# Attention, then two expert layers, on one core: the opening of the attention written out as a sequence of its own

## The chip, the core and the metric

The kernel runs on one core of a Trainium2 chip. TensorE (PE in the rows) multiplies matrices into PSUM. VectorE (DVE), ScalarE (ACT) and GpSimd (POOL) work on SBUF; the first two also read PSUM. SyncE (SP), ACT and POOL issue transfers, which run on 16 DMA engines. Each engine works through its own list in order and waits on semaphores for the others. The metric is the device time of one execution in microseconds (us); the median of several runs is compared.

## What is computed

Inputs q, k, v have shape (2, 8, 576, 64): 16 heads of 576 positions by 64 numbers; s has shape (2, 8, 576). The result of the attention goes through two expert layers (1152 tokens, 8 experts, 512 to 1024 to 512). Only the attention is touched here:

```python
scores = scale * np.matmul(q, k.transpose(0, 1, 3, 2))
s_pos = np.maximum(s, 0.0)
cum = np.cumsum(s_pos, axis=-1)
bias = -(cum[:, :, :, None] - cum[:, :, None, :])
scores = np.where(causal, -1000000000.0, scores + np.minimum(bias, 0.0))
scores = scores - np.max(scores, axis=-1, keepdims=True)
attn = np.exp(scores)
attn = attn / (np.sum(attn, axis=-1, keepdims=True) + 1e-09)
return np.matmul(attn, v)
x = _moe_ref(x=x, **moe_kwargs)      # first expert layer
return _moe2_ref(x=x, **moe2_kwargs) # second expert layer
```

## The kernel before, in words

The 16 heads come as 8 pairs n, heads 2n and 2n+1; a head's 576 positions are five tiles of 128 (the last holds 64). Four things happen to a head m:

- **Turning** (T, TE). The pair's q and k are split into two float16 numbers each, high on ACT (`split_q`, `split_k`, line 401) and low on DVE (line 441). TensorE transposes the tiles into PSUM (line 452), ACT copies them out (line 409): `AL` is the turned k, `AR` the turned q. `AL` is also copied to the lower half of `BLS` by a transfer on SP's queue (line 463); the upper half of `BLS` holds a fixed pattern of 32-column groups.
- **Maxima** (M, D, G). TensorE forms the scores in four pieces u = 0 to 3 (`m_pe`, line 476; the causal mask is added by line 478 from `mask_ij`), DVE adds the decays `CB[m]` and takes the row maxima into `rm` (`m_dve`, line 488). `CB[m]` is row m of the running sums `cum13`, the same on all 128 partitions. ACT rounds `rm` (`q_dve0`, line 494, task G0), POOL forms the difference `ng` to the references `refb` and splits it into `QB` (`q_dve1`, task G1). A piece's PSUM tile is one of two, so piece u+2 waits for DVE's maximum of piece u.
- **Exponentials** (Q, QE, E). `QB` is turned on TensorE and copied by DVE into `BR`; TensorE forms the scores again, turned (lines 528 to 531), ACT takes the exponential into `pf` (line 536).
- **Values** (P, V, R, X). DVE and POOL split `pf` into two halves (lines 403 and 414), TensorE multiplies with v (lines 559 to 564), DVE divides; per pair the rows are turned and multiplied with the gate weights of the first expert layer.

One loop runs over m from -7 to 18. In each step two written lists, one for even and one for odd m (`ORDER`), set the order in which these tasks are issued for different heads: E for m, Q for m+1, M, D and G for m+3, T for m+5, K for the pair (m+7)/2. The steps of negative m are the fill: they run the same lists with the tasks whose head does not exist yet left out. Beside the lists stand `filled(m)` (paddings, set by POOL), `references()` at m = -5 (from `cum13`, the references `refb` and the exponents' offsets `XB`) and `groups()` at m = -3 (the pattern in `BLS[0]`, made by DVE, and five transfers from POOL's queue that copy it to the other five `BLS`). `cum13` is a scan on DVE over `s` (lines 303 and 305); it is written to DRAM, and `cum_load(m)` reads row m back onto 128 partitions, 288 KB a head.

SP's queue takes, in program order, s, k and q of each pair (each in three transfers: `load_qkv`, lines 207 and 208), the decays, v, the gate weights and the copies into `BLS`. At m = 10 the gate of the first half of the tokens is taken, and from there on weights of the expert layers arrive; the two expert layers follow.

Of the kernel before, what the change touches and what calls it, by code (L numbers as in the profile page):

```python
# [21 lines left out]
def tile_attention_moe_moe(ctx: ExitStack, tc: tile.TileContext, q, k, v, s, wg1, w1a, w2a, capacity,  # L22
                           wg2, w1b, w2b, out, dbg=None):
    nc = tc.nc
# [196 lines left out]
    load_qkv(KF, k, 1)  # L221

    for l in (KF, QF):
        nc.gpsimd.memset(l[0][64:, 4], 0.0)
    gi = sp.tile([P, S], I32, name="gi")

# [4 lines left out]
    VH = [ap.tile([P, NS16, 2, D + 1], F16, name=f"vh{i}") for i in range(3)]  # L231
    ALS, ARS = ([ap.tile([P, SW], F16, name=f"{n}{i}") for i in range(6)] for n in ("al", "ar"))
    BLS = [ap.tile([P, SW], F16, name=f"bl{i}") for i in range(6)]
    xt = ap.tile([P, 2, SW], F16, name="xt")
    RMS = [ap.tile([P, NT], F32, name=f"rm{i}") for i in range(4)]
# [5 lines left out]
    def filled(m):  # L241

        put = nc.gpsimd.memset
        if m == -6:
            for l in (KF, QF):
                put(l[1][64:, 4], 0.0)
        if m == -5:
            nc.gpsimd.iota(gi[64:96], pattern=[[1, S]], base=0, channel_multiplier=-32)
        if m in (-4, -2):
            for i in range(3):  # L250
                for x in (ALS, ARS, BLS):
                    put(x[i + 3 * (m == -2)][:, S:], 0.0)
        if m == -4:
            for x in RMS:
                put(x, 0.0)
            for l in (KF, QF):
                put(l[2][64:, 4], 0.0)
        if m == -3:
            for i in range(2):
                put(VF[i][64:, 4], 0.0)  # L260
                put(VF[i][:, :, :, D:], 32.0)
            for x in VH:
                put(x[:, :, :, D:], 32.0)
            put(QB[0][:, :, :, D:], 0.0)
        if m == -2:
            put(QB[1][:, :, :, D:], 0.0)
        if m in (-2, -1):
            i = m + 2
            put(PFS[i][:, NCOL:], 0.0)
            put(PFS[i][64:, NCOL - 64:NCOL], 0.0)  # L270
            for l in (PHS, PLS):
                put(l[i][:, 2 * S - P:], 0.0)
        if m == -1:
            put(QB[2][:, :, :, D:], 0.0)
            put(zero[:, :DM + E + 1], 0.0)
            put(zero[:, DM + E + 1:], 2e6)
        if m == 0:
            for i in range(2, 4):
                put(VF[i][64:, 4], 0.0)
                put(VF[i][:, :, :, D:], 32.0)  # L280
# [51 lines left out]
    magic = ap.tile([P, 1], F32, name="magic")  # L332
    nc.vector.memset(magic, MAGIC)

    def groups():
        nc.vector.tensor_scalar(g1[64:96], gi[64:96], 0.0, -1024.0, op0=OP.is_ge, op1=OP.mult)
        for r in (64, 96):
            nc.vector.scalar_tensor_tensor(BLS[0][r:r + 32, :S], gi[64:96], 31.0, g1[64:96], op0=OP.is_le, op1=OP.mult)
        for x in BLS[1:]:
            nc.gpsimd.dma_start(x[64:, :S], BLS[0][64:, :S])  # L340

    def references():
# [1673 lines left out]
```

## Time and profile before

| what | value |
|---|---|
| median of 3 runs | 454.91 us (452.60 to 456.92) |
| the profiled execution, its own time | 451.49 us |
| its span, first to last instruction | 449.7 us |
| PE / DVE / ACT / POOL busy, share of the span | 88% / 74% / 58% / 42% |
| scan done (start of the attention's own work on DVE) | 5.47 us |
| first maximum of head 0 / 1 / 2 / 3 on DVE | 13.69 / 20.10 / 25.90 / 31.49 us |
| first exponential's matmul, head 0 | 28.74 us |
| last of the attention's values | about 141 us |

The times are of one execution. A row of the timeline gives the start, the duration, the engine and line, what is written from what, and in square brackets how long the engine stood idle before it and who released it. Busy shares are means over stages with different limits, so the opening is read by itself.

### The profile page before, as it was taken

What the parts mean: (1) busy time and instruction counts of PE and PEld (TensorE: products, weight loads), DVE (VectorE), ACT (ScalarE), POOL (GpSimd) and SP (SyncE); (2) the same over time, 40 slices, a digit from 0 to 9 for tenths busy, and PEclk for the clock granted to TensorE, in tenths of its full rate; (3) what the DMA queues carried; (4) which work ended last, traced back from release to release, by engine and by line L of the source; (5) the groups of instructions that cost most, each with busy time, mean ns of one, the idle gap of its engine ahead of it and who ended that gap; (6) DMA issues with size and microseconds to landing.
All of it is one profiled execution on the core that took longest, in us unless ns stands there. A gap on an engine that the chain in (4) does not pass through costs nothing. (4 is left out here: it accounts for less than half of the span.)

```text
span 449.7 us, 13971 instructions
## 1 busy us (share of the span) xinstructions
PE 397.8 (88%) x5378; PEld 366.1 (81%) x5378; DVE 330.9 (74%) x954; ACT 262.2 (58%) x473; POOL 190.9 (42%) x306
## 2 busy tenths in 40 slices
PE   1679999975987799999999999868979999999992
PEld 1447888864876699999999999737969999999991
DVE  7889999984667466776778894767598878877620
ACT  4457898752574165555556854533486776675631
POOL 4387888867470512052044081420254233334221
PEclk9979999998899999999999999998999999999997
DMA  7797999777924769999999691096999898899411
GB/s 156 168 214 171 224 227 199 189 180 243 362 30 158 250 202 318 355 347 339 336 341 377 101 175 21 20 264 155 331 366 332 272 336 279 260 336 315 143 42 32
DMA packets 94399, 103.04 MB, mean 229 GB/s; under 512 B 56136, under 2 KB 63304, under 8 KB 94323
## 3 DMA queue, kind: packets, MB, share of 16 engines
q1 hardware_dynamic: 88931, 91.85, 70.9%
q0 software_dynamic: 4192, 9.91, 7.4%
q8 instruction: 44, 0.72, 0.7%
q10 hardware_dynamic: 1200, 0.30, 0.3%
q14 instruction: 32, 0.26, 0.2%
HBM read 81.42 MB, written 14.59 MB: 213 GB/s over the span
## 5 line engine op out<-in xcount | busy, mean ns | idle before, releaser
L164 DVE TENSOR_TENSOR wl<-wf,wh 128x1024 bf16<-128x1024 f32 x64 | 78.0, 1237 | 20.8 <-ACT wh L160 19.2
L160 ACT ACTIVATE wh<-wf 128x1024 f16<-128x1024 f32 x64 | 65.7, 1050 | 16.8 <-issue 9.1
L937 PE MATMUL A<-xt,wl 128*128 128x144 f16 (+4 forms) x288 | 59.5, 231 | 0.0
L935 PE MATMUL A<-xt,wh 128*128 128x144 f16 (+4 forms) x288 | 59.5, 231 | 0.0
L936 PE MATMUL A<-xt,wh 128*128 128x144 f16 (+4 forms) x288 | 59.5, 231 | 0.0
L992 PE MATMUL C<-h,wf 128*128 128x160 f32 (+7 forms) x544 | 58.3, 269 | 0.0
L1107 POOL DMA_INDIRECT x2d<-xo,tix x14 | 22.9, 1637 | 74.1 <-DVE l L1124 26.4
L937 PEld LDWEIGHTS <-wl 128*128 128x128 bf16 x512 | 50.2, 98 | 1.5 <-issue 1.5
L936 PEld LDWEIGHTS <-wh 128*128 128x128 f16 x512 | 50.2, 98 | 1.4 <-issue 0.9
L935 PEld LDWEIGHTS <-wh 128*128 128x128 f16 x512 | 50.3, 98 | 1.2 <-PE pM L652 1.0
L536 ACT ACTIVATE pf<-pE,XB 128x512 f32<-128x512 f32 (+4 forms) x80 | 36.8, 514 | 12.5 <-PE pE L531 12.4
L488 DVE CUSTOM_DVE_ANT_0 junk<-pM,cb 128x128 f16<-128x128 f32 (+4 forms) x80 | 32.2, 431 | 11.7 <-PE pM L478 11.0
L1885 POOL DMA_INDIRECT out_dram<-x2f,tok x14 | 16.8, 1198 | 55.9 <-ACT h L943 24.9
L414 POOL TENSOR_TENSOR pl<-pf,ph 128x512 f16<-128x512 f32 x30 | 35.5, 1194 | 9.2 <-DVE ph L403 7.5
L476 PE MATMUL pM<-al,ar 128*128 128x128 f16 (+2 forms) x96 | 27.9, 330 | 11.6 <-DVE rm L488 7.0
L164 DVE TENSOR_TENSOR wf<-wf,wf 128x1024 bf16<-128x1024 f32 x30 | 35.7, 1219 | 2.6 <-ACT wf L160 2.6
L992 PEld LDWEIGHTS C<-h,wf 128*128 128x128 f32 x256 | 36.2, 190 | 0.0
L1454 POOL DMA_INDIRECT xg<-x2d,tok x16 | 24.0, 1498 | 23.4 <-PE A L1152 11.0
L1865 PE MATMUL C<-h,wf 128*128 128x144 f32 (+1 forms) x312 | 32.0, 257 | 0.0
L160 ACT ACTIVATE wf<-wf 128x1024 f16<-128x1024 f32 x30 | 31.3, 1052 | 0.0
L559 PE MATMUL pog<-vf,pf 128*128 128x65 f32 x180 | 29.4, 287 | 0.0
L937 PE MATMUL C<-xt,wl 128*128 128x144 f16 x128 | 24.6, 226 | 0.0
(415 smaller groups left out, 1188.8 us busy)
## 6 DMA issues: line engine op xcount, KB each, us to landing
wf<-in_moe_w_dram SPq DMA_DIRECT2D x128, 512.0 KB
xd<-zero SPq DMA_DIRECT2D x18, 257.0 KB
cb<-cumd SPq DMA_DIRECT2D x16, 288.0 KB
x2d<-zero SPq DMA_DIRECT2D x9, 260.5 KB
kf<-in_k_dram SPq DMA_DIRECT2D x16, 128.0 KB
vf<-in_v_dram SPq DMA_DIRECT2D x16, 128.0 KB
qf<-in_q_dram SPq DMA_DIRECT2D x14, 128.0 KB
bl<-al SPq DMA_DIRECT2D x16, 72.0 KB
```

Of the source, the lines that this page charges most:

```text
L160: nc.scalar.activation(hi, src, AF.Copy)
L164: nc.vector.tensor_sub(lo, src, hi)
L414: (nc.gpsimd if ENG[name][i % 2] == "P" else nc.vector).tensor_sub(o, x, y)
L476: nc.tensor.matmul(o, AR[m][:, t * P:(t + 1) * P], AL[m][:, j0:j1], start=True, stop=not diag)
L488: nc.vector.tensor_tensor_reduce(junk[:w, :j1 - j0], o, CB[m][:w, j0:j1], 1.0, r if t == 4 and j0 == 0 else -3e38, OP.add, OP.max, r)
L536: nc.scalar.activation(d, o, AF.Exp, bias=x, scale=2.0 ** -13)
L559: nc.tensor.matmul(o, pf[:, c:c + P], VF[n % 4][:, j, h], start=False, stop=j == t)
L935: nc.tensor.matmul(ph[:, g], wh[:, c, fs], xt[:, c], start=c == 0, stop=False)
L936: nc.tensor.matmul(ph[:, g], wh[:, c, fs], xt[:, 4 + c], start=False, stop=False)
L937: nc.tensor.matmul(ph[:, g], wl[:, c, fs], xt[:, c], start=False, stop=c == 3)
L992: nc.tensor.matmul(py[:, g], a[:, f, d], b[:, f], start=k == 0, stop=k == len(terms) - 1)
L1865: nc.tensor.matmul(py[:, g], a[:, f, d], b[:, f], start=k == 0, stop=k == len(terms) - 1)
```

## The change

The loop starts at m = -1. What its steps -7 to -2 did is written out as straight code ahead of it, in another order and with other means:

- k of a pair comes in one transfer: partition p holds nine neighbouring rows of the pair, 2304 bytes in one piece, where before 256-byte rows were spread over three transfers. The pair is turned by nine transposes instead of ten, and ACT puts the columns back in place with two strided copies (a first of 640, a second of 512 elements a partition) that serve both heads.
- The decays of heads 0, 1 and 2 no longer come from DRAM: a float32 matmul spreads the row of `cum13` over 128 partitions (512 and 64 columns), and ACT copies it from PSUM (`cum_pe`). Heads 3 to 15 still load them.
- The references' work on DVE follows the scan at once, ahead of k's and q's low halves; `refb` is made by ACT. The masks are made by DVE after that, where before they stood ahead of the scan. The group pattern is made ahead of the scan, one piece instead of two; two POOL transfers (5 and 6 heads, 32 partitions each) copy it.
- Paddings are merged into fewer, larger memsets and stand early on POOL. v of pairs 0 and 1 and both layers' gate weights are loaded from POOL's queue instead of SP's, between these paddings.
- `G0` (the rounding of `rm`) moves behind the last maximum, `D3`, in both lists and in the fill. Head 0's turned q is copied by DVE instead of ACT.

```diff
@@ load_qkv, filled (was called by m, now by steps)
+        if l is KF:
+            queue.dma_start(x, r.rearrange("h (q t) d -> (h q) t d", t=NK))
+            return
...
+        if step == 0:
+            put(ABL[:, :, S:], 0.0)
+            put(RMA, 0.0)
+            put(QF[1][64:, 4], 0.0)
+            put(VHS[:, :, :, :, D:], 32.0)
...
+            nc.gpsimd.dma_start(wgf, wg1.rearrange("(c p) e -> p c e", p=P))
+            for n in range(2):
+                load_qkv(VF, v, n, nc.gpsimd)
+            nc.gpsimd.dma_start(wg2f, wg2.rearrange("(c p) e -> p c e", p=P))
+            put(QB[0][:, :, :, D:], 0.0)
+            put(QF[2][64:, 4], 0.0)
+        if step == 1:
+            for r, i in ((64, 1), (96, 0)):
+                nc.gpsimd.dma_start(ABL[r:r + 32, 12 + i:, :S], BLS[0][64:96, None, :S].to_broadcast([32, 6 - i, S]))
...
-    load_qkv(QF, q, 1)
-    cum_load(0)
-    cum_load(1)
...
+    def cum_pe(m):
+        CB[m] = aw.tile([P, S], F32, name="cb", bufs=3)
+        for c0, c1 in ((0, 512), (512, S)):
+            pb = psE.tile([P, 512], F32, name="pE")[:, :c1 - c0]
+            nc.tensor.matmul(pb, identf[:NH, m:m + 1].to_broadcast([NH, P]), cum13[:, c0:c1], start=True, stop=True)
+            nc.scalar.activation(CB[m][:, c0:c1], pb, AF.Copy)
...
-        for r in (64, 96):
-            nc.vector.scalar_tensor_tensor(BLS[0][r:r + 32, :S], gi[64:96], 31.0, g1[64:96], op0=OP.is_le, op1=OP.mult)
-        for x in BLS[1:]:
-            nc.gpsimd.dma_start(x[64:, :S], BLS[0][64:, :S])
...
-        nc.vector.tensor_scalar(refb, pr, MAGIC, None, op0=OP.add)
+        nc.scalar.activation(refb, pr, AF.Identity, bias=magic)
@@ t_evac
-        moved("AL", m, AL[m][:, :S], ps[0][:, :S])
-        moved("AR", m, AR[m][:, :S], ps[1][:, :S])
+        for p, t0 in zip(ps[:-1], (0, NT)):
+            t1 = min(t0 + NT, NK)
+            nc.scalar.activation(ABL[:, m % 6:m % 6 + 2, :S].rearrange("p h (q t) -> p h q t", t=NK)[:, :, :, t0:t1],
+                                 p[:, :(t1 - t0) * P].rearrange("p (t h q) -> p h q t", h=2, t=t1 - t0), AF.Copy)
+        if m:
+            moved("AR", m, AR[m][:, :S], ps[-1][:, :S])
+        else:
+            raw_copy(AR[m][:, :S], ps[-1][:, :S])
@@ the opening
-    for m in range(-7, NH + 3):
+    filled(0)
+    references()
+    split_k(0)
+    split_rest()
+    split_q(0)
+    masks()
+    split_rest()
+    cum_pe(0)
+    refs = references_pe()
+    turned0 = t_pe(0)
+    split_k(1)
+    t_evac(0, turned0)
+    split_rest()
+    references_out(*refs)
+    filled(1)
+    maxima(0, {0: lambda: turn(1), 1: lambda: split_q(1), 2: lambda: cum_pe(1)})
...
+    gate_weights()
+    split_v(0)
+    maxima(1, {0: lambda: turn(2), 1: split_rest, 2: lambda: (split_k(2), cum_pe(2))})
+    cum_load(3)
+    load_v(2)
+    split_v1(0)
+    split_rest()
+    split_q(2)
+    turn(3)
+    split_rest()
+    filled(3)
...
+    for m in range(-1, NH + 3):
```

What stands in the lists of three engines is shown at the three places that matter most. On DVE, before, right behind the scan (the second row) come k's and q's low halves of pair 0 and k's of pair 1, and only then the references:

```order
L303 TENSOR_SCALAR srow<-srow 16x576
L305 SCALAR_TENSOR_TENSOR cum<-ones_row,srow 16x576
L333 MEMSET magic 128x1
L441 SCALAR_TENSOR_TENSOR ka<-kf_109,ka 128x10x64
L403 COPY qa<-qa 128x10x64
L441 SCALAR_TENSOR_TENSOR qb_132<-qf_108,qa 128x10x64
L441 SCALAR_TENSOR_TENSOR ka<-kf_112,ka 128x10x64
L344 TENSOR_SCALAR ref_263<-cum 16x18
```

Now the group pattern (`abl<-gi`) stands ahead of the scan and the references right behind it; k's low half comes last of these:

```order
L295 SCALAR_TENSOR_TENSOR abl<-gi,g_152 32x576
L298 TENSOR_SCALAR srow<-srow 16x576
L300 SCALAR_TENSOR_TENSOR cum<-ones_row,srow 16x576
L341 TENSOR_SCALAR ref_211<-cum 16x18
L342 TENSOR_SCALAR ref_211<-ref_211 16x18
L343 CAST refh<-ref_211 16x18
L345 TENSOR_TENSOR r8l<-ref_211,refh 16x18
L346 CAST refh<-r8l 16x18
L347 TENSOR_TENSOR selc<-ident 64x16
L348 SCALAR_TENSOR_TENSOR ones_row<-ref_211,cum 16x576
L443 SCALAR_TENSOR_TENSOR ka<-kf_109,ka 128x9x64
```

On TensorE, between the third and the fourth piece of head 0's scores, two float32 matmuls now stand (they spread head 1's decays; the last row is the fourth piece, whose maximum ends head 0):

```order
L491 MATMUL pM<-abl 128x512
L493 LDWEIGHTS identk
L493 MATMUL pM<-mask_ij,identk 128x128
L321 MATMUL pE<-cum,identf 128x512
L321 MATMUL pE<-cum,identf 128x64
L491 LDWEIGHTS abl
L491 MATMUL pM<-abl 128x512
```

On POOL, ahead of head 0's difference to the references (`ng`, in both lists), eight transfers now stand that were on SP's queue, and the two copies of the pattern. The rows start behind the last padding of v's second pair:

```order
L259 DMA wgf<-in_moe_w_gate_dram 128x4x8
L211 DMA vf_110<-in_v_dram 128x4x64 x2
L212 DMA vf_110<-in_v_dram 64x2x64
L211 DMA vf_113<-in_v_dram 128x4x64 x2
L212 DMA vf_113<-in_v_dram 64x2x64
L262 DMA wg2f<-in_moe_w_gate_dram 128x4x8
L263 MEMSET qb_131 128x10x64
L264 MEMSET qf_114 64x128
L267 DMA abl<-abl 32x5x576
L267 DMA abl<-abl 32x6x576
```

Before, only paddings stood ahead of that difference on POOL, and the pattern's copies came behind it:

```order
L263 MEMSET vh_137 128x4
L264 MEMSET qb_132 128x10x64
L500 TENSOR_TENSOR ng<-rm_157,refb 128x90
L403 CAST qb_132<-ng 128x5x18
L414 TENSOR_TENSOR qb_132<-ng,qb_132 128x5x18
L340 DMA bl_151<-bl_150 64x576
```

## Rows read from the trace of the kernel before

**Rows 1.** Busy time by stretch: length, five engines (instructions), granted clock, DMA share, GB/s.
```profile
5.47:31.49 26.02, 15.78 (x130) 11.59 (x130) 20.48 (x60) 13.07 (x27) 12.69 (x41) 0.87 0.85 185
31.49:90.94 59.45, 57.89 (x849) 49.44 (x848) 57.44 (x201) 49.19 (x113) 49.06 (x72) 1.00 0.87 202
27.30:30.70 3.40, 3.40 (x22) 2.35 (x22) 2.40 (x6) 2.81 (x5) 2.95 (x11) 0.50 0.99 228
```

**Rows 2.** Timeline of DVE in the opening: start, duration, what; idle before, released by.
```profile
1.60 0.17 DVE L62 MEMSET ones<- 128x128 f16 x1
...
3.01 1.07 DVE L303 TENSOR_SCALAR srow<-srow 16x576 f32<-16x576 f32 x1 [0.18 <-DMA srow<-in_s_dram]
4.12 1.35 DVE L305 TENSOR_TENSOR_SCAN cum<-ones_row,srow 16x576 f32<-16x576 f32 x1
...
6.90 0.82 DVE L441 SCALAR_TENSOR_TENSOR ka<-kf,ka 128x640 f16<-128x640 f32 x1 [1.43 <-ACT ka L401]
...
11.77 0.46 DVE L363 TENSOR_SCALAR refb<-pM 128x288 f32<-128x288 f32 x1 [0.79 <-PE pM L360]
...
13.69 0.29 DVE L488 CUSTOM_DVE_ANT_0 junk<-pM,cb 128x128 f16<-128x128 f32 x1 [0.46 <-issue]
...
17.85 0.50 DVE L336 TENSOR_SCALAR g<-gi 32x576 f32<-32x576 int32 x1
18.38 1.58 DVE L338 SCALAR_TENSOR_TENSOR bl<-gi,g 32x576 f16<-32x576 int32 x2
...
23.43 1.82 DVE L405 TENSOR_SCALAR vf<-vf 128x640 f32<-128x640 f32 x1
...
31.49 0.29 DVE L488 CUSTOM_DVE_ANT_0 junk<-pM,cb 128x128 f16<-128x128 f32 x1 [1.42 <-PE pM L478]
...
35.91 0.77 DVE L405 TENSOR_SCALAR vf<-vf 128x640 f32<-128x640 f32 x1
...
48.19 0.48 DVE L405 TENSOR_SCALAR vf<-vf 128x640 f32<-128x640 f32 x1
```

**Rows 3.** Timeline of PE: the references, the turn at m = -1, and float32 matmuls.
```profile
10.54 0.66 PE L357 MATMUL pM<-identf,ones_row 16*128 16x16 f32 x5 [1.51 <-DVE ones_row L347]
11.13 0.60 PE L360 MATMUL pM<-refh,selc 64*128 64x18 f16 x16
...
12.70 0.31 PE L476 MATMUL pM<-al,ar 128*128 128x128 f16 x1
...
27.29 0.59 PE L476 MATMUL pM<-al,ar 128*128 128x512 f16 x1
27.68 0.74 PE L452 MATMUL pT<-ident,ka 128*128 128x128 f16 x5
...
28.74 0.63 PE L528 MATMUL pE<-br,bl 128*128 128x512 f16 x1
...
110.35 1.52 PE L559 MATMUL pog<-vf,pf 128*128 128x65 f32 x6
111.67 0.63 PE L476 MATMUL pM<-al,ar 128*128 128x512 f16 x1
```

**Rows 4.** Timeline of ACT: a copy of turned k in the fill; the end of an even step (m = 2).
```profile
8.54 0.65 ACT L409 ACTIVATE al<-pT 128x576 f16<-128x576 f16 x1 [0.41 <-PE pT L452]
...
46.42 0.30 ACT L494 ACTIVATE rm<-rm,magic 128x5 f32<-128x5 f32 x1
...
...
49.28 0.84 ACT L536 ACTIVATE pf<-pE,XB 128x64 f32<-128x64 f32 x2 [0.79 <-PE pE L531]
```

**Rows 5.** Timeline of POOL: transfers that it issues, and head 0's difference.
```profile
17.18 0.85 POOL L500 TENSOR_TENSOR ng<-rm,refb 128x90 f32<-128x90 f32 x1 [11.39 <-DVE rm L488]
...
20.28 2.85 POOL L340 DMA_DIRECT2D bl<-bl  x5 [0.93 <-DVE wgh L370]
...
105.77 0.98 POOL L706 DMA_INDIRECT xd<-XR,slot  x1 [0.30 <-issue]
107.06 0.93 POOL L706 DMA_INDIRECT xd<-XR,slot  x1 [0.30 <-issue]
```

More of the change, by code (lines that the diff above doesn't have):

```diff
@@ L221, in tile_attention_moe_moe @@
     load_qkv(KF, k, 1)
-    for l in (KF, QF):
-        nc.gpsimd.memset(l[0][64:, 4], 0.0)
+    load_qkv(QF, q, 1)
     gi = sp.tile([P, S], I32, name="gi")
+    nc.gpsimd.iota(gi[64:96], pattern=[[1, S]], base=0, channel_multiplier=-32)
+    nc.gpsimd.memset(QF[0][64:, 4], 0.0)
     SW = NT * P
@@ L239, in tile_attention_moe_moe, with filled @@
     XSS = [ap.tile([P, NT, 2, D], F32, name=f"xs{i}") for i in range(2)]
-    def filled(m):
+    def filled(step):
         put = nc.gpsimd.memset
[L244 to L258, printed above, removed]
-            for i in range(2):
[L260 to L274, printed above, removed]
@@ L276, in filled @@
             put(zero[:, DM + E + 1:], 2e6)
[L277 to L280, printed above, removed]
+        if step == 3:
+            for x in VF[2:]:
+                put(x[64:, 4], 0.0)
+                put(x[:, :, :, D:], 32.0)
             put(xt[:, :, S:], 0.0)
@@ L353, in references, with references_pe @@
         nc.vector.tensor_copy(refh[32:32 + NH], r8l)
-        pb = psM.tile([P, NT, NH], F32, name="pM")
+        nc.vector.tensor_tensor(selc, ident[:64, :NH], ident[:64, 32:32 + NH], OP.add)
+        nc.vector.scalar_tensor_tensor(xrow.rearrange("e (g w) -> e g w", w=32),
+                                       ref8[:, :, None].to_broadcast([NH, G, 32]), -1024.0,
+                                       cum13.rearrange("e (g w) -> e g w", w=32), op0=OP.mult, op1=OP.add)
+    def references_pe():
+        pr = pog[:, :NH * G].rearrange("p (h g) -> p h g", g=G)
+        pb = pog[:, NH * G:NH * G + NT * NH].rearrange("p (t h) -> p t h", h=NH)
+        for h in range(NH):
+            nc.tensor.matmul(pr[:, h], selc[:, h:h + 1].to_broadcast([64, P]), refh, start=True, stop=True)
         for t in range(NT):
@@ L456, in t_pe @@
         n, h, b, hh = heads(m)
-        return [transposed(KA[n][:, :, h]), transposed(QA[n][:, :, h])]
+        ps = []
+        for t0 in (0, NT) if h == 0 else ():
+            p = psT.tile([P, SW], F16, name="pT")
+            for t in range(t0, min(t0 + NT, NK)):
+                nc.tensor.transpose(p[:, (t - t0) * P:(t - t0 + 1) * P], KA[n][:, t], ident)
+            ps.append(p)
+        return ps + [transposed(QA[n][:, :, h])]
     def t_evac(m, ps):
+        n, h, b, hh = heads(m)
         AL[m], AR[m] = ALS[m % 6], ARS[m % 6]
-        moved("AL", m, AL[m][:, :S], ps[0][:, :S])
-        moved("AR", m, AR[m][:, :S], ps[1][:, :S])
+        for p, t0 in zip(ps[:-1], (0, NT)):
[6 more added lines that the diff above has]
+            raw_copy(AR[m][:, :S], ps[-1][:, :S])
         nc.sync.dma_start(BLS[m % 6][:64, :S], AL[m][:64, :S])
@@ L758, in tile_attention_moe_moe, with maxima, turn @@
     ORDER = [
-        "E0 Q E1 K X1 M0 D0 V0 M1 V1 D1 X QE M2 VS XE E3 P0 D2 P1 QS E2 V2 R0 R1 G0 M3 T R2 D3 XG VT TE L LG G1 LV S".split(),
-        "E0 VS M0 V0 Q D0 M1 E1 D1 P0 P1 V1 X1 E3 K E2 QE M2 V2 D2 R0 M3 X T R1 G0 LG XE TE R2 D3 QS L S G1 VT XG LV".split(),
+        "E0 Q E1 K X1 M0 D0 V0 M1 V1 D1 X QE M2 VS XE E3 P0 D2 P1 QS E2 V2 R0 R1 M3 T R2 D3 G0 XG VT TE L LG G1 LV S".split(),
+        "E0 VS M0 V0 Q D0 M1 E1 D1 P0 P1 V1 X1 E3 K E2 QE M2 V2 D2 R0 M3 X T R1 LG XE TE R2 D3 G0 QS L S G1 VT XG LV".split(),
     ]
     made = {}
-    for m in range(-7, NH + 3):
+    def maxima(m, between):
+        for u in range(4):
+            m_dve(m, m_pe(m, u))
+            if u in between:
+                between[u]()
+        q_dve0(m)
+        q_dve1(m)
+    def turn(m):
+        t_evac(m, t_pe(m))
+    filled(0)
[14 more added lines that the diff above has]
+    maxima(0, {0: lambda: turn(1), 1: lambda: split_q(1), 2: lambda: cum_pe(1)})
+    nc.vector.tensor_scalar(mask_ji, jp, 0.0, -60000.0, op0=OP.is_lt, op1=OP.mult)
+    load_pair(3)
+    filled(2)
+    gate_weights()
[9 more added lines that the diff above has]
+    filled(3)
+    setup.close()
+    XRF = at.enter_context(tc.tile_pool(name="xrp", bufs=1)).tile([P, B, NT, ROW // 2], F32, name="XR")
+    XRP += [XRF, XRF.bitcast(F16)]
+    xrf = XRF.rearrange("p b t r -> p (b t) r")[:, :, DM:]
+    for b in range(B):
+        nc.gpsimd.iota(xrf[:, b * NT:(b + 1) * NT, 1:2], pattern=[[P, NT], [0, 1]], base=b * S + 1,
+                       channel_multiplier=1, allow_small_or_imprecise_dtypes=True)
+    for m in range(-1, NH + 3):
         if 1 < m + 5 < NH:
```

86 lines of the change are left out of this document (38 added, 48 removed).

## The prediction

> **What bounds the kernel now.** I read the page for the shares, then the busy time by stretch, then the timelines of DVE, PE, ACT and POOL side by side over the first 50 us, and last how the opening passes into the steady heads. From 31.49 to 90.94 us DVE works 57.44 of 59.45 us and PE 57.89 [rows 1]: nothing there has room to catch up, so whatever the opening gains or loses is carried on. The opening, from the end of the scan (4.12 + 1.35 = 5.47) to the first maximum of head 3 (31.49) [rows 2], is 26.02 us, of which DVE works 20.48 [rows 1] and stands 5.54. PE works 15.78 of it, and much of that at the lower of its two clocks: ten transposes of 128 columns take 28.74 - 27.68 = 1.06 us [rows 3], 0.106 each, which is 128 columns at 1.2 GHz, and the clock granted from 27.3 to 30.7 is 0.50 [rows 1]. So the opening is DVE's list plus the places where DVE waits for a chain through PE and ACT. I forecast when the first maximum of head 3 comes now, and let the rest follow unchanged.
>
> **DVE's start.** Before, DVE took up s at 3.01 after a wait of 0.18 for its transfer [rows 2]. Now the group pattern stands ahead: 0.50 for the comparison and half of 1.58 for one piece [rows 2], 1.29 in all. Its other constants are done at 1.60 + 0.17 [rows 2], two tiny memsets follow, so s is taken up at about 3.2. The scan ends at 5.47 + 0.2 = 5.67.
>
> **DVE's own work** from there to head 3, against 20.48:
> - the pattern leaves the stretch: 0.50 + 1.58 = 2.08 less; `refb` goes to ACT: 0.46 less [rows 2];
> - four low halves of k have 576 elements for 640, a tenth of 0.82 each [rows 2]: 0.33 less;
> - v of pair 0, scaled in place (line 405), took 1.82 while POOL set paddings; the same instruction takes 0.77 and 0.48 later [rows 2]. The paddings now stand elsewhere; I take 0.77, 1.05 less, and keep 0.48 and 1.82 as bounds;
> - three masks and the selector come in from ahead of the scan, priced like the memset of that size, 4 x 0.17, and head 0's turned q is copied by DVE, priced like 288 words from PSUM, 0.46 [rows 2]: 1.14 more.
> In sum 20.48 - 3.92 + 1.14 = 17.70.
>
> **DVE's waits**, one by one:
> - *Head 0's turned q.* PE starts with the decays. A float32 matmul of 65 columns takes (111.67 - 110.35)/6 = 0.22 at the lower clock [rows 3], so 576 columns 1.95; the references' matmuls 0.60 and their transposes 11.13 - 10.54 = 0.59 [rows 3], fourteen transposes 1.48. The last ends at 5.67 + 4.62 = 10.29. DVE meanwhile does the references (about 1.9), k low, q's copy, two masks, q low: ready at about 9.7. Wait 0.7.
> - *First maximum.* k's turned columns leave through ACT's two strided copies, 640 and 512 elements, where the known copy has 576 contiguous ones in 0.65 [rows 4]; I price them by size, 1.3 for both, done at 10.8. Maxima follow the first matmul by 13.69 - 12.70 = 0.99 [rows 2, 3]: 11.85, where before it was 13.69. DVE has q's copy and k low of pair 1 to fill this: wait 0.3.
> - *Between the second and the third maximum* DVE copies pair 1's q, whose high half ACT makes only behind head 1's copy: 0.3.
> - *Fourth maximum of head 0.* PE spreads head 1's decays first, 1.95 at the lower clock, half of it at the upper: wait 1.4 or 0.3. PE has been at work since 5.7 with few gaps; I take 0.8.
> - *Head 1*: the same with head 2's decays, and fourteen transposes, but DVE has q low between: 0 to 1.3, taken 0.3.
> - *End of the fill.* From the fourth piece of head 2 (27.29) to 31.49 were 4.20 [rows 2, 3]; PE turns a pair's k and one q now (14 transposes for 10), 0.42 more, 4.6; DVE covers about 2.5 with two maxima, a copy and k low. The clock granted there was 0.50 [rows 1], and I expect no better: wait 2.1; at the upper clock next to none, 0.2. I take 2.2 with 0.1 for q's copy of pair 2.
>
> Sum 0.7 + 0.3 + 0.3 + 0.8 + 0.3 + 2.2 = 4.6. The first maximum of head 3 comes at 5.67 + 17.70 + 4.6 = 27.97, **3.5 us earlier**. With every wait and v's scaling at its better end it is 5.67 + 17.41 + 1.8 = 24.9 (6.6 earlier), at the worse 5.67 + 18.75 + 6.3 = 30.7 (0.8).
>
> **What I cost at nothing.** k's single transfers: the decays of the first three heads and 256-byte pieces leave the queues; ACT's wait for k is not on DVE's chain. ACT's spreading copies stand beside DVE's maxima. In steady pairs PE has one transpose fewer and DVE 0.08 less per pair, but ACT, working 49.19 of 59.45 [rows 1], now turns three PSUM tiles in one step, and head m+1's Q needs the first of them back: about as much as is saved. G0 behind D3 makes ACT wait in even steps from 46.42 to about 48.2 (v's scaling at 48.19 comes right behind that maximum on DVE) [rows 2, 4]; one copy of 0.65 fewer follows, and 0.79 of idle at 49.28 takes most of the rest [rows 4]. If that cover were gone, 0.5 us a pair over five pairs, 2.5.
>
> **Rival 1: POOL's transfers come too late (slower).** Eight transfers now stand ahead of head 0's difference `ng`, six of 512 pieces and two of 128. Five of 64 took 2.85, 0.57 each; a scatter of 128 rows 0.98, of 64 rows 0.93, so 0.8 ns a row more [rows 5]. By this a large one costs 0.57 + 448 x 0.0008 = 0.93 and all eight 6.8. With paddings until about 5, two pattern copies (1.3) and 3.5 of paddings, POOL reaches `ng` at about 17, as before (17.18) [rows 5]. It is needed by 20.6, when its turn must precede the copy `br` on DVE. So 3.9 us are free: above 1.6 us a large transfer every 0.1 costs 0.6; at 2.2 the gain is gone, at 2.9 it is 1% slower. Priced by the piece, 0.57/64 = 8.9 ns, a large one costs 4.55 and all 29.6: 22.8 - 3.9 - 3.5 = 15.4 slower, 470. I take the scatters' slope, since the cost hardly changed there with the rows, but they are another instruction.
> POOL and DVE also hinder one another: v's scaling lost 1.82 - 0.48 = 1.34 beside POOL's paddings [rows 2]. If each of the eight transfers lost as much, 10.7 - 3.9 - 3.5 makes 3.3 slower, 458.2. Against it is that the five at 20.28 ran beside DVE's maxima at 0.57 [rows 5]. The Trainium skill (SBUF — State Buffer, section "SBUF: two separate sides") speaks against this change: a transfer issued from GpSimd waits while DVE holds the shared port, 620 ns becoming 3100 in its example. By that figure eight would take 24.8, an estimate that ends 10.6 us slower; the five rows here do not show it.
>
> **Rival 2: ACT becomes the bound.** If strided reading from PSUM costs twice its size, 1.3 more a pair, ACT's 9.9 of a pair's 12 us (49.19 of 59.45 [rows 1], which hold nearly ten heads) become 11.3 with 0.1 for the larger count, and with G0's 1.8 of waiting it exceeds the pair by 1.1: over five pairs 5.5 - 3.5, 2.0 slower, 456.9. It decides from about 0.6 a pair on. No row shows such a copy.
>
> **Rival 3: the gain is swallowed.** Between 90.94 and the first expert a scatter, zero fills and weights pace the work; if one of them is not shifted with the heads, nothing is left: 454.9. Against it speaks that each follows a gate that depends on the heads.
>
> **How the numbers follow.** The forecast has 0.63, rival 1 0.20 (0.12 by the pieces, 0.08 by the hindrance, of which the skill's rule is the stronger form), rival 2 0.07, rival 3 0.10. The profiled execution would take 451.49 - 3.5 = 448.0. Its own time is 3.4 below the median of the runs; against the median I say 454.91 - 3.5 = **451.4**. What a measurement of this kernel can tell from no change is about 1%, 4.5 us. Gains of 0.8 to 6.6 pass that in some four cases of nine: faster 0.27. Same has the forecast's other 0.36, 0.07 of rival 1, 0.05 of rival 2 and rival 3: 0.58. Slower 0.15. The range goes from 448.3, all waits at their better end, up to 457.5, which takes in rivals 2 and 3 and the mild end of rival 1, and leaves out some 0.17. The forecast alone has 448.3 to 454.1.
>
> **What would show it.** The scan at about 5.7, first maxima of head 0 at 11.9 and of head 3 at 28; line 405's first at 0.8; two PE stretches of decays between 1.0 and 2.0; the strided copies at 0.7 and 0.6; POOL's large transfers at 0.9 to 1.6 and `ng` at 17. Wrong would be: `ng` behind 20.6, with DVE standing ahead of `br`; ACT without idle time from 35 us on; or head 3 early but the first scatter of the gate not earlier by the same amount.

## The result, and the profile after

The changed kernel takes 454.39 us (median of 20 runs, 452.46 to 458.24), the kernel before 453.48 us on the same chip (20 runs). The medians lie 0.9 us apart; the ratio of the runs is 1.0063, 95% interval 1.0040 to 1.0086, which would be 2.9 us. The two agree on the sign and not on the size. Both lie inside the 1% that the prediction called no change, and on the other side of what I forecast (451.4, that is 3.5 faster). The profiled execution took 453.29 us, its span 451.4; before it was 451.49 and 449.7.

The same three stretches as in [rows 1] (length, five engines with their instructions, granted clock, DMA share, GB/s):

```profile
5.47:31.49 26.02, 21.99 (x144) 14.12 (x144) 19.49 (x64) 15.01 (x33) 16.86 (x54) 1.00 0.66 143
31.49:90.94 59.45, 56.29 (x809) 47.47 (x810) 56.22 (x192) 46.87 (x108) 44.31 (x56) 1.00 0.88 205
27.30:30.70 3.40, 3.01 (x35) 2.23 (x36) 3.09 (x12) 1.88 (x4) 2.26 (x21) 1.00 0.20 50
```

In the opening TensorE works 6.2 us more than before. In the steady heads, where the prediction expected nothing, TensorE and DVE both do less in the same time (809 and 192 instructions for 849 and 201): they stand more.

DVE in the opening, the rows that answer to [rows 2] (start, duration, what; idle before, released by):

```profile
2.26 1.72 DVE L294 TENSOR_SCALAR g<-gi 32x576 f32<-32x576 int32 x1
4.02 0.75 DVE L295 SCALAR_TENSOR_TENSOR abl<-gi,g 32x576 f16<-32x576 int32 x1
...
5.36 1.34 DVE L300 TENSOR_TENSOR_SCAN cum<-ones_row,srow 16x576 f32<-16x576 f32 x1
...
11.90 0.46 DVE L392 TENSOR_SCALAR abl<-pT 128x288 int32<-128x288 int32 x1 [1.11 <-PE pT L454]
...
13.39 0.29 DVE L503 CUSTOM_DVE_ANT_0 junk<-pM,cb 128x128 f16<-128x128 f32 x1 [0.37 <-PE pM L493]
...
17.84 0.74 DVE L503 CUSTOM_DVE_ANT_0 junk<-pM,cb,rm 64x512 f16<-64x512 f32 x1 [1.79 <-PE pM L491]
...
23.79 0.74 DVE L503 CUSTOM_DVE_ANT_0 junk<-pM,cb,rm 64x512 f16<-64x512 f32 x1 [1.48 <-PE pM L491]
...
24.47 0.48 DVE L407 TENSOR_SCALAR vf<-vf 128x640 f32<-128x640 f32 x1
...
30.95 0.29 DVE L503 CUSTOM_DVE_ANT_0 junk<-pM,cb 128x128 f16<-128x128 f32 x1 [0.56 <-PE pM L493]
```

The scan ends at 6.70 and the first maximum of head 3 stands at 30.95, 0.54 earlier than before, where 3.5 were forecast. The two largest waits are those for the fourth maximum of heads 0 and 1. TensorE shows why (a row of x4 is four matmuls, two for the 512 columns and two for the 64):

```profile
14.23 0.61 PE L491 MATMUL pM<-abl 128*128 128x512 f16 x1
...
14.87 2.39 PE L321 MATMUL pE<-cum,identf 16*128 16x512 f32 x4
17.20 0.71 PE L491 MATMUL pM<-abl 128*128 128x512 f16 x2
...
20.82 2.39 PE L321 MATMUL pE<-cum,identf 16*128 16x512 f32 x4
23.15 0.61 PE L491 MATMUL pM<-abl 128*128 128x512 f16 x1
...
27.57 0.39 PE L491 MATMUL pM<-abl 128*128 128x512 f16 x1 [1.68 <-DVE rm L503]
```

The fourth piece starts only when the decays of the next head are spread, 2.33 us later. TensorE is at the lower of its two clocks there, though the rows above say 1.00: a matmul of 512 columns takes 0.61 (0.59 in [rows 3], where [rows 1] has a granted clock of 0.50), and from 27.57 on 0.39. POOL, against [rows 5]:

```profile
2.10 0.57 POOL L297 MEMSET ones_row<- 16x576 f32 x1
2.62 1.05 POOL L252 MEMSET abl<- 128x1152 f16 x1
...
6.49 1.55 POOL L211 DMA_DIRECT2D vf<-in_v_dram  x2
...
8.61 1.76 POOL L211 DMA_DIRECT2D vf<-in_v_dram  x2
...
19.01 0.34 POOL L515 TENSOR_TENSOR ng<-rm,refb 128x90 f32<-128x90 f32 x1 [2.26 <-ACT rm L509]
```

The large transfers cost 0.78 to 0.98 each (0.78 and 0.88 in the mean of the two pairs shown), and POOL waited 2.26 us for ACT ahead of `ng`: the transfers were not late.

From head 3 to head 13 the first maxima lie 63.53 us apart (30.95 to 94.48), before 60.23 (31.49 to 91.72). So 3.30 us were lost in the stretch that I had counted as nothing. Head 13 is 2.76 us late, the first scatter of the second gate 2.23 (151.68 for 149.45), the end of the span 1.7. Most of the loss sits in three even steps (m = 4, 6, 8), which take 0.93, 0.90 and 0.91 longer: from the first maximum of head 7 to that of head 8 it takes 7.87 us where it took 6.94. The place in the kernel before, at m = 4:

```profile
57.16 1.16 POOL L414 TENSOR_TENSOR pl<-pf,ph 128x512 f16<-128x512 f32 x1
...
57.55 1.06 DVE L403 CAST ph<-pf 128x512 f16<-128x512 f32 x1
...
57.65 0.73 ACT L401 ACTIVATE qa<-qf 128x640 f16<-128x640 f32 x1
...
58.53 0.31 DVE L403 COPY qa<-qa 128x640 f16<-128x640 f16 x1
...
58.75 1.16 POOL L414 TENSOR_TENSOR pl<-pf,ph 128x512 f16<-128x512 f32 x1 [0.43 <-PE pM L476]
```

and now:

```profile
56.69 1.16 POOL L416 TENSOR_TENSOR pl<-pf,ph 128x512 f16<-128x512 f32 x1
...
57.49 0.65 DVE L405 CAST ph<-pf 128x512 f16<-128x512 f32 x1
...
57.59 0.73 ACT L403 ACTIVATE qa<-qf 128x640 f16<-128x640 f32 x1
...
58.28 1.16 POOL L416 TENSOR_TENSOR pl<-pf,ph 128x512 f16<-128x512 f32 x1 [0.43 <-DMA qf<-in_q_dram]
58.35 1.26 DVE L405 COPY qa<-qa 128x640 f16<-128x640 f16 x1 [0.22 <-ACT qa L403]
```

Both DVE's copy of q's high half (QD, behind ACT's QH) and POOL's second difference `pl` stand behind DVE's cast `ph`. Before, the cast itself was held beside the first `pl` (1.06), so that QH was long done and the copy came first, in 0.31. Now POOL is 0.47 earlier, the cast takes 0.65, and QH, which is only 0.06 earlier, comes too late by 0.07: `pl` starts at 58.28, the copy at 58.35, and it takes 1.26, until just behind the end of `pl` (59.44). That happens three times (1.26, 1.23, 1.24 for 0.31 to 0.33): 2.76 us. The shorter cast gives nothing back, because DVE then stands 0.22 for QH: counted from head 7's first maximum (54.62 before, 54.46 now) the copy starts 3.91 behind it before and 3.89 now, so the step's 0.93 is the copy's.

### The profile page after: what moved, and what is told of

Same layout as the page of the kernel before. It is cut to its first block, busy times and chain, and to the rows that moved or that the text cites. A ratio compares the mean times of both kernels' runs of the same rounds, so it can differ in the third digit from the quotient of the medians.

```text
span 451.4 us, 13907 instructions
## 1 busy us (share of the span) xinstructions
PE 406.0 (90%) x5382; PEld 369.5 (82%) x5382; DVE 331.3 (73%) x952; ACT 263.2 (58%) x479; POOL 193.0 (43%) x287
## 5 line engine op out<-in xcount | busy, mean ns | idle before, releaser
L491 PE MATMUL pM<-abl 128*128 128x128 f16 (+2 forms) x96 | 28.2, 334 | 6.3 <-ACT pf L551 3.3
L1504 POOL DMA_INDIRECT xg<-x2d,tok x16 | 22.6, 1412 | 23.5 <-PE A L1202 10.9
L573 PEld LDWEIGHTS pog<-vf,pf 128*128 128x128 f32 x180 | 24.7, 199 | 0.0
```

The lines of the kernel that those rows point to most:

```text
L491: nc.tensor.matmul(o, AR[m][:, t * P:(t + 1) * P], AL[m][:, j0:j1], start=True, stop=not diag)
L573: nc.tensor.matmul(o, pf[:, c:c + P], VF[n % 4][:, j, h], start=False, stop=j == t)
```

## The experiments

**Three theories of the steady loss.** C: DVE's copy of q is held by POOL's `pl`, as just read. G: the rounding behind the last maximum is the cause; ACT now stands for it, as a row of the waits from 31 to 91 us says (total, times, longest):

```profile
ACT rm L509 <- DVE rm L503: 9.1, 5, 2.1
```

K: the turn of a whole pair, longer on TensorE and ACT in the odd steps, has that price. The runs below were timed in four batches (e1 to e4, e5 to e8, e9 to e12, e13 to e16), each on a chip of its own, against the kernel before there (median 445 to 446 us). The columns behind the ratio are from one profile of each.

| run | what | ratio (95% interval) | first max. of head 3 | head 3 to 13 | copy at m = 4 |
|---|---|---|---|---|---|
| before, first profile | | | 31.49 | 60.23 | 0.31 |
| changed, first profile | | 1.0063 (1.0040-1.0086) | 30.95 | 63.53 | 1.26 |
| e1 | changed, rounding back | 1.0030 (0.9992-1.0069) | 31.02 | 63.63 | 1.27 |
| e2 | changed, copy on ACT | 0.9966 (0.9928-1.0004) | 28.71 | 60.64 | on ACT |
| e3 | before, rounding late | 1.0024 (0.9987-1.0061) | 30.84 | 61.84 | 0.32 |
| e4 | before, pair turn | 1.0089 (1.0053-1.0125) | 29.91 | 63.65 | 1.26 |
| e5 | changed, QH early | 0.9959 (0.9929-0.9988) | 30.95 | 60.64 | 0.33 |
| e6 | e5, decays loaded | 0.9938 (0.9909-0.9966) | 29.43 | 60.61 | 0.33 |
| e7 | e6, pattern behind | 0.9977 (0.9952-1.0002) | 29.01 | 60.63 | 0.33 |
| e8 | changed, copy as two-input | 1.0095 (1.0061-1.0129) | 29.90 | 66.04 | 1.76 |
| e9 | e4, QH early, QH twice | 1.0068 (1.0041-1.0094) | 29.66 | 61.53 | 0.33 |
| e10 | before, QH late | 1.0152 (1.0117-1.0188) | 33.65 | 65.44 | 0.95 |
| e11 | e5, decays behind 4th piece | 0.9987 (0.9947-1.0027) | 28.67 | 60.62 | 0.33 |
| e12 | e6, head 4's turn ahead | 0.9902 (0.9869-0.9934) | 28.33 | 60.62 | 0.33 |
| e13 | changed, again | 1.0025 (0.9986-1.0065) | 30.96 | 63.55 | 1.27 |
| e14 | before, one execution | | 32.01 | 60.88 | 0.31 |
| e15 | e4, QH early | 1.0018 (0.9986-1.0051) | 31.00 | 60.69 | 0.33 |
| e16 | e12, rounding back | 0.9926 (0.9893-0.9960) | 28.72 | 60.67 | 0.33 |

**e1: the rounding back at its old place.** The two lists of the kernel before, in the changed one:

```diff
-... R2 D3 G0 XG ...   /  -... R1 LG XE TE R2 D3 G0 QS ...
+... R1 G0 M3 T R2 D3 XG ...  /  +... R1 G0 LG XE TE R2 D3 QS ...
```

> The changed kernel with the rounding (G0) back at its old place, ahead of the last maximum; nothing else is touched. Theory C: the changed kernel loses its time in three even steps (at 58, 72 and 85 us), where DVE's copy of q's high half (line 405, 640 elements) takes 1.23 to 1.26 instead of 0.31 because it starts just behind the start of POOL's difference pl; the rounding has no part in it. Then the copies stay at 1.2 and the ratio to the kernel before at 1.006 (about 454.4). Theory G: the rounding behind the last maximum makes ACT stand 1.1 to 2.1 us in each even step, and that is what delays the pairs. Then a pair goes from 13.35 back to 12.4 us and the ratio to 1.000 or below. Theory K (the turn of a whole pair in odd steps, with two strided copies of 1.39 together) expects 1.006.

ACT's waits for the maximum fell to 0.6 and less, and nothing else moved: 63.63, copies of 1.27, 1.20, 1.19. G falls as the cause in the changed kernel.

**e2: the copy on ACT.** Both parities of QD go from DVE to ACT:

```diff
-... QH="AA", QD="DD", last="DD" ...
+... QH="AA", QD="AA", last="DD" ...
```

> The changed kernel with q's second copy (QD) made by ACT, right behind its high half, instead of DVE. Theory C: DVE has no such copy to be held; the pair goes from 13.35 us to 12.4 or a little less, 2.8 us come back and the ratio to the kernel before is 1.000 to 0.998 (450.5 to 451.5 against 454.4). ACT gets 0.5 to 0.7 a pair, which lies in its 2.1 us of waiting. Theories G and K: ACT has even more to do ahead of the rounding or the turn, so the loss stays or grows: 1.006 to 1.010.

The pair is back at 12.37 us and the ratio 0.6 to 1.0% under the two of the changed kernel (1.0025 in e13, and 1.0063). In the profile some of it is the opening (head 3 at 28.71), where TensorE ran at the upper clock from 13.6 to about 20 us in this execution.

**e3 and e4: one part of the change in the kernel before.** e3 has the changed lists (e1's diff the other way round), e4 k's single transfer, the nine transposes and the two strided copies; all else is the kernel before.

```diff
@@ e4: load_qkv, t_pe and t_evac as in the changed kernel
+            queue.dma_start(x, r.rearrange("h (q t) d -> (h q) t d", t=NK))
...
-        return [transposed(KA[n][:, :, h]), transposed(QA[n][:, :, h])]
+        return ps + [transposed(QA[n][:, :, h])]
```

> The kernel before with the rounding (G0) behind the last maximum, as in the changed one; nothing else. Theory G: ACT's turned copies of an even step come 2 us later and each pair loses 0.9, so 1.006 to 1.010 of the kernel before. Theory C: DVE's copy of q stays right behind its cast and at 0.31, and the time within 0.2% of the kernel before, unless the shift moves POOL against DVE. Theory K: 1.000.

> The kernel before with k of a pair in one transfer, turned as nine tiles in odd steps and written by ACT's two strided copies; its fill, decays and rounding as they were. Theory K: the longer turn delays the odd step's copies and with them the pair, 1.006. Theories C and G: the odd steps have room for it and the ratio is 1.000 (a little below, for one transpose and 0.08 of DVE's work fewer a pair), with the copies of q at 0.31.

e4 alone makes all of the loss, e3 leaves the copy at 0.32. Late rounding alone costs 1.6 us on the way to head 13 in its profile, by longer odd steps (6.28 and 6.27 for 5.36 and 5.40) that the even ones make up only in part, but its ratio can't be told from 1. The mechanism in e4 is in its distances at m = 4, taken from head 7's first maximum: POOL's first `pl` starts 2.23 behind it (before 2.54), ACT's QH ends 3.87 behind it (before 3.76). In the changed kernel they are 2.23 and 3.86, in e3 2.55 and 3.80. So the longer odd steps bring POOL 0.3 ahead and ACT 0.1 back, and the order of copy and `pl` turns round.

**e5: q's high half one place earlier on ACT.** A task of its own, ahead of the exponential E3:

```diff
-... VS XE E3 P0 D2 P1 QS ...
+... VS XE QH E3 P0 D2 P1 QS ...
```

> The changed kernel with q's high half (QH) on ACT one place earlier in even steps, ahead of the exponential E3 (0.30); DVE's copy (QD) stays where it was. Theory C: in the changed kernel the copy missed by 0.07 us: q's high half is there at 58.35, POOL's difference pl starts at 58.28. With 0.3 earlier the copy starts right behind its cast, ahead of pl, and takes 0.31; a pair goes from 13.35 to about 12.4 us, first maxima of heads 7 and 13 lie 37 apart (they were 40.0), and the ratio to the kernel before is 0.996 to 1.000. Theory K (the longer turn itself) and theory G (the late rounding) leave it at 1.006 and 13.35, since neither is touched; by the kernel before with late rounding, G alone could keep 0.4 a pair, ratio 1.001 to 1.003.

```profile
57.41 0.74 ACT L403 ACTIVATE qa<-qf 128x640 f16<-128x640 f32 x1
...
58.18 0.33 DVE L405 COPY qa<-qa 128x640 f16<-128x640 f16 x1
58.30 1.23 POOL L416 TENSOR_TENSOR pl<-pf,ph 128x512 f16<-128x512 f32 x1 [0.43 <-DMA qf<-in_q_dram]
```

0.18 us earlier on ACT give back 2.9 us: the copy is ahead of `pl`, and of the 3.30 lost 0.41 is left. The opening of this execution equals that of the changed kernel's profile to 0.01 us, so the difference is this move's alone. C stands.

**e8: the copy written with two inputs.** From pair 3 on, in the same place:

```diff
+nc.vector.scalar_tensor_tensor(fl(qa)[:, :, D:], fl(qa)[:, :, :D], 1.0, fl(qa)[:, :, :D], op0=OP.mult, op1=OP.max)
```

> The changed kernel with DVE's copy of q from pair 3 on written as an operation with two inputs (scalar_tensor_tensor, the maximum of the half with itself); its place is unchanged, behind POOL's start of pl. Theory C in its form: what holds the copy is that a one-input operation of SBUF on DVE (copy, cast, scaling) stands while POOL works there, and two-input ones beside pl did not (qb's low half 0.81 everywhere). Then this one takes 0.7 to 0.8 at 58, 72 and 85 us in place of 1.2, and about 0.45 a pair comes back, the ratio 1.002 to 1.004. If every DVE operation is held there, it takes 1.3 or more and the ratio stays at 1.006.

My extension, that only one-input operations are held, fell:

```profile
33.40 0.81 DVE L429 SCALAR_TENSOR_TENSOR qa<-qa 128x640 f16<-128x640 f16 x1
33.56 1.66 POOL L416 TENSOR_TENSOR pl<-pf,ph 128x512 f16<-128x512 f32 x1 [0.36 <-DVE ph L405]
...
58.23 1.16 POOL L416 TENSOR_TENSOR pl<-pf,ph 128x512 f16<-128x512 f32 x1 [0.43 <-DMA qf<-in_q_dram]
58.31 1.76 DVE L429 SCALAR_TENSOR_TENSOR qa<-qa 128x640 f16<-128x640 f16 x1 [0.23 <-ACT qa L403]
```

Whoever starts second waits: at 33 us DVE first, in 0.81, and POOL takes 1.66 for 1.16; at 58 us POOL first, and DVE takes 1.76. Maxima, which read PSUM, are not held (0.69 at 56.87 in the changed kernel, beside the first `pl`). The Trainium skill (SBUF — State Buffer, section "SBUF: two separate sides") states this rule: DVE and GpSimd share one pair of ports, given whole to whichever starts first, a DVE operation counting when it runs in a two-port mode or has two inputs in SBUF, the latter only against a GpSimd operation that reads SBUF. These rows agree, in both directions.

**e10: the collision without the change.** The kernel before, with QH one place later, behind E2:

```diff
-... XE E3 P0 D2 P1 QS E2 V2 ...
+... XE E3 P0 D2 P1 E2 QH QS V2 ...
```

> The kernel before with nothing changed but q's high half on ACT one place later in even steps, behind the exponentials E2 (0.82). Its own lateness makes DVE's copy start about 0.5 later (59.1 for 58.53 in that step). Theory C: it then stands behind pl (58.75 to 59.91) and takes 1.0 to 1.3 in place of 0.31, so an even step loses 1.2 to 1.4 and the ratio is 1.008 to 1.010, with nothing of the change in the kernel. If the copy is not held by pl, the step loses 0.5 and the ratio is 1.003 to 1.004; if DVE has slack there, 1.000.

```profile
61.50 1.05 DVE L403 CAST ph<-pf 128x512 f16<-128x512 f32 x1
...
62.69 1.16 POOL L414 TENSOR_TENSOR pl<-pf,ph 128x512 f16<-128x512 f32 x1 [0.42 <-PE pM L484]
63.08 0.95 DVE L403 COPY qa<-qa 128x640 f16<-128x640 f16 x1 [0.53 <-ACT qa L401]
```

0.53 of waiting and 0.64 of being held in the step: a pair takes 13.54, 1.14 more than before, and all five even steps lose. Only those steps are read: this kernel, like e9, made q's high half twice for the first three pairs (its early task ran beside the old one), which delayed the opening, and so the ratio is above what was expected.

**e9 and e15: does the pair turn have a price of its own?** e4 with QH early as in e5; in e9 with that doubling, in e15 without.

> The kernel before with the turn of a whole pair (as in the run of that alone, which was 1.0089 and had the copy of q at 1.20 to 1.26) and, in addition, q's high half one place earlier on ACT. Theory C: the turn costs time only because it puts POOL's difference pl ahead of DVE's copy; with the half 0.3 earlier the copy takes 0.31 to 0.33, the way from head 3's first maximum to head 13's goes from 63.65 us to about 60.5 (before: 60.23), and the ratio is 0.998 to 1.002. Theory K: the longer turn has a cost of its own; 62 or more remain, ratio 1.005 or above.

> The kernel before with the turn of a whole pair and q's high half one place earlier in every even step, made once for each pair. Theory C: the turn costs through the held copy alone; head 3 to head 13 in 60.3 to 60.8 us and the ratio 0.997 to 1.002. Theory K: the turn has a price of its own; 1.004 or more as in the run with the doubling, and then a stretch other than the steady pairs must show it.

e9 looked like K (1.0068), but its copies were at 0.33, and its profile doesn't show the extra time in the pairs: the steps up to head 7 are 0.85 longer than in e15, but head 3 is 1.34 earlier, and head 13 comes at 91.19, in e15 at 91.69. It falls behind e15 only at the second gate, where DVE waits 1.75 us for TensorE (0.30 in e15). Whether the doubling does that isn't shown. e15 has 60.69 to head 13 and a ratio of 1.0018: the turn costs through the held copy, and some 0.4 us beside it.

**e6, e11, e12, e7: where the opening's gain went.** e6 loads the decays of heads 1 and 2 again, on SP behind pair 2's k and q:

```diff
+    cum_load(1)
+    cum_load(2)
...
-    maxima(0, {..., 2: lambda: cum_pe(1)})
+    maxima(0, {...})
-    maxima(1, {..., 2: lambda: (split_k(2), cum_pe(2))})
+    maxima(1, {..., 2: lambda: split_k(2)})
```

> As the kernel with q's high half early, and the decays of heads 1 and 2 loaded from DRAM as before the change; only head 0's are spread by TensorE. If the opening lost its gain at the two places where the fourth maximum waited 1.79 and 1.48 behind the spreading (2.35 us each at the lower clock), first maximum of head 3 comes at 27.7 to 28.5 instead of 30.95 in a profile at the lower clock (less, 1.0 to 1.5, where TensorE is at its upper clock early), and the time falls by as much, 1 to 3 us or 0.2 to 0.7% against the kernel with q's high half early alone. Rival: TensorE at the lower clock is the bound of the opening anyway, or the steady heads do not carry the lead on; then the difference is under 0.1%.

The two waits are gone, head 3 comes 1.52 earlier (29.43), and the first scatter of the second gate 1.56 earlier (142.09 for 143.65): up to there what the opening gains is carried on. The medians, 442.60 and 444.13, differ by as much, but the intervals overlap, and the two profiles don't show it at the end (span 444.6 for e5's 441.2). The 1.52 may not be the loading's alone either, since TensorE rose to its upper clock near 21.5 us in e6 and by 27.5 in e5. The expected 27.7 wasn't reached since a wait at the end of the fill took the place of the others:

```profile
29.43 0.29 DVE L513 CUSTOM_DVE_ANT_0 junk<-pM,cb 128x128 f16<-128x128 f32 x1 [2.15 <-PE pM L503]
```

e11 leaves the spreading on TensorE, but behind the fourth piece:

```diff
-    maxima(0, {..., 2: lambda: cum_pe(1)})
+    maxima(0, {..., 3: lambda: cum_pe(1)})
-    maxima(1, {..., 2: lambda: (split_k(2), cum_pe(2))})
+    maxima(1, {..., 2: lambda: split_k(2), 3: lambda: cum_pe(2)})
```

> The changed kernel with q's high half early, and the decays of heads 1 and 2 still spread by TensorE, but behind the fourth matmul piece of the head ahead in place of in front of it. If the place was the fault, the waits of 1.79 and 1.48 at the fourth maxima go, and of the 2.35 us of spreading only what DVE can't cover comes back at the next head's first maximum, 1.0 to 1.8 each: first maximum of head 3 0.5 to 1.5 earlier than 30.95 at the lower clock, 0.1 to 0.3% under the kernel with q's half early alone. If TensorE's 2.35 us are the fault wherever they stand, head 3 comes at 30.5 to 31 and the time is unchanged; only loading them (29.43) helps.

Inconclusive: in its profile TensorE was at the upper clock when both spreadings ran (1.29 for 2.39), so head 3 at 28.67 says little of the place, and its interval overlaps e5's.

e12 sets head 4's nine turns of k, in the step m = -1, into TensorE's idle time ahead of the third piece of head 2 (its q's turn stays behind the fourth piece):

```diff
+        if m == -1:
+            names = [x for x in names if x != "T"]
+            names.insert(names.index("M2"), "T")
+            names.insert(names.index("M3") + 1, "TQ")
```

> The kernel with q's half early and the decays loaded, and in the last step ahead of the steady ones head 4's nine turns of k set ahead of the third matmul piece of head 2, where TensorE stood 2.30 us for DVE (22.15 to 24.46). The wait ahead of head 3's first maximum (2.15) falls by 0.7 to 1.0; head 3 at 28.4 to 28.7 and the time 0.2% under 0.9938, about 0.992. Rival: the tiles of PSUM that the turn holds delay head 0's turned references or head 2's pieces, and nothing is gained.

The wait fell from 2.15 to 1.69, less than expected, and head 3 came at 28.33, with TensorE at the upper clock from 14.2 to about 24 us. e16 below, where it rose near 21 as in e6 and the rounding is early as well, has the wait at 0.98 and head 3 at 28.72. 0.9902 is the lowest ratio of all runs; its interval overlaps e6's and lies below 1 and below both of the changed kernel.

e7 moves the group pattern (`g1` and `BLS[0]`, and POOL's two copies of it) behind head 0's maxima:

```diff
     maxima(0, {...})
+    pattern()
```

> As the last, and the group pattern (lines 294 and 295, 2.5 us ahead of the scan) moved behind head 0's maxima, its spreading on POOL behind that. If the pattern beside POOL's paddings made the scan end at 6.70 instead of about 5.5, the scan ends 0.9 to 1.3 earlier, head 0's first maximum comes at 12.1 to 12.5 for 13.39; head 3's gains the same less what the pattern (1.3) costs in its new place: 0 to 1.0. Rival: the copy of s on DVE is held by the same paddings, or head 0 waits for q's transfer (7.87), so that the scan or the first maximum gains under 0.4.

```profile
2.78 1.21 DVE L296 TENSOR_SCALAR srow<-srow 16x576 f32<-16x576 f32 x1 [0.54 <-DMA srow<-in_s_dram]
4.09 1.35 DVE L298 TENSOR_TENSOR_SCAN cum<-ones_row,srow 16x576 f32<-16x576 f32 x1
...
16.02 0.45 DVE L340 TENSOR_SCALAR g<-gi 32x576 f32<-32x576 int32 x1
```

The comparison takes 0.45 away from the paddings, 1.72 beside them; now the scaling of s is held in its stead (1.21 for 0.45). The scan ends 1.26 earlier, head 0's first maximum comes 1.26 earlier, head 3's 0.42. The median didn't follow (443.56 for 442.60); the intervals of e6 and e7 overlap.

**e13, e14, e16: what was open at the end.**

> The changed kernel itself, timed on the chip of the other runs, where the kernel before takes 445 us and not 453. If the loss belongs to the program (three held copies, 2.8 us), the ratio is 1.005 to 1.008 again and head 3 to head 13 take 63.5 us; if it belonged to the first chip, 1.000 to 1.003.

> The kernel before, for its profile on this chip. Copies of q 0.31 to 0.33, head 3 to head 13 in 60.2 us as in the first profile; the stand of 4.5 us at 110 us, which the other profiles of this chip don't have, is gone here too if it belonged to that execution and not to the program.

> The fastest kernel so far (q's half early, decays loaded, head 4's turns of k ahead; 0.9902) with the rounding back at its old place ahead of the last maximum. ACT's waits of 0.97 to 2.04 for the last maximum go. If DVE and TensorE set the pairs, which stand at 12.37, nothing changes: 0.990, within 0.1%. If late rounding had a price left, 0.3 to 0.4 a pair comes back, 0.986 to 0.987.

e13 has the copies and 63.55 again; its ratio is lower here (1.0025), with an interval that holds both 1.000 and the first chip's 1.006. Part of that may be the kernel before: in e14, an execution of it on this chip, two odd steps stood for late transfers of decays, the second (at 81.00) for 0.39, the first for longer:

```profile
68.65 0.29 DVE L488 CUSTOM_DVE_ANT_0 junk<-pM,cb 128x128 f16<-128x128 f32 x1 [1.14 <-DMA cb<-cumd]
```

The first profile had no such wait. How often that comes wasn't tried. The stand of 4.5 us that e14's expectation asks about is gone there; both profiles of the first chip have it (DVE waits 4.54 ahead of 110.25 before, 4.52 ahead of 112.96 changed), so it is no part of their difference. e16: with the copy free, the rounding's place is worth nothing (60.67 against 60.62).

## Why the prediction was wrong, point by point

- **"Steady state counted as nothing"** is the step that failed, and it decided the sign. I compared sums of work: one transpose fewer, 0.08 less on DVE, a wait of ACT behind 0.79 of cover. Those sums held but for some 0.4 us (e5, e15); ACT's waits of up to 2.1 us cost nothing in the changed kernel (e1, e16), though late rounding alone took 1.6 on the way in the kernel before (e3). What I did not look at was which of two engines comes first where both use SBUF: moving POOL by 0.3 and ACT by 0.1 turned a margin around, at 0.9 a pair in three pairs. The rows for it were there before: the casts `ph` at 1.06 beside `pl`, and v's scaling at 1.82 beside paddings, which I had even read [rows 2]. I used that hindrance for POOL's transfers (rival 1) and not for the steady pairs.
- **Rival 2** (ACT bound by strided copies) had the right place, the turn, and nearly the right loss (2.0 us for 1.8 between the two profiled executions), but by another mechanism, so that is luck. The strided copies took 1.34 to 1.39 for both, as priced (1.3), and ACT kept idle time.
- **The scan**, 5.67 forecast, was at 6.70: the comparison ahead of it 1.72 where [rows 2] has 0.50. I had taken it at its undisturbed price although the change set POOL's paddings beside it. DVE's list also began 0.4 later (`ones` at 2.01 for 1.60), and the scaling of s, at 0.45 for 1.07, gave 0.62 back.
- **DVE's own work**, 17.70 forecast, was 17.72, the busy time from 6.70 to 30.95; v's scaling in it was 0.48. The rest of these 24.25 us is 6.53 of standing, 6.27 of it in waits that rows show.
- **DVE's waits**, 4.6 forecast, were 6.27: head 0's turned q 1.11 and its first maximum 0.37 (for 1.0 together), the fourth maxima 1.79 and 1.48 (for 0.8 and 0.3), the rest of the heads 0.96 (for 0.3), the end of the fill 0.56 (for 2.2). The sum of the decays was mis-sized: 2.3 at the lower clock, not 1.95, and TensorE stayed at that clock until 27.5. With the decays loaded and the lower clock at the end of the fill, that wait was 2.15 (e6), as the term had it. Scan 1.03, work 0.02 and standing 1.93 make the 2.98 by which head 3 came later than 27.97.
- **That the lead is carried on** was right up to the second gate (e6: 1.52 at head 3, 1.56 at its first scatter). For the end there are e12 and e16, with medians 3.3 and 3.5 us under the kernel before and head 3 at 28.33 and 28.72. Rival 3 falls.
- **Rival 1** falls: transfers at 0.78 to 0.98 and POOL waiting for ACT ahead of `ng`. No run here shows the starved transfers of the Trainium skill's example (SBUF — State Buffer, "SBUF: two separate sides"). The lock that the same section describes did decide, but between two engines' operations.

With QH one place earlier (e5) the change gives 0.9959, by that ratio 1.8 us of the 3.5 forecast (0.9 by the medians); with the decays loaded as well (e6) 0.9938, and with head 4's turn ahead (e12) 0.9902.

## What to carry to other kernels

Where DVE and POOL both run copies, casts or two-input operations in SBUF, read the order in which they start, not only their durations: here an operation that came 0.07 us second waited out the whole of the first. When a change shifts one of them by a few tenths against the others, look at each such meeting in the steady loop and give the shorter one a margin; moving its producer one place forward cost nothing here (e5). A price taken from a row is the price beside what ran there: ask what will run beside it now.

## What the runs showed of the hardware that I had not expected

- A held operation shows as busy, not as waiting: the copies of q count 1.26 us of DVE work, the paddings' neighbour 1.72. Only a comparison of the same form elsewhere (0.31, 0.45) shows the loss.
- TensorE ran at its lower clock through most of an opening in which it was busy 4.97 of 5.00 us (13 to 18), while the record of the granted clock says 1.00 there: 512 columns took 0.61, as at the granted 0.50 in the kernel before (0.59), later 0.39. When it rises differs between executions of one program: by 27.57 us in the first profile of the changed kernel, behind a stand of 1.68, at 20.2 in e13's, and in e12, whose list on TensorE is the same up to there, at 14.2. Prices from such a stretch need both levels.
